# The opening of a Fourier and mixture kernel: batch 0's first stage stored and relaid in groups, half of w1 converted later

## The chip, the cores and the metric

The kernel runs on one core of a Trainium2 chip. The metric is the device time of one execution in microseconds (us). Before the change it is 980.48 us, the median of 3 runs (980.14 to 981.08).

## What is computed

```python
def _attn_ref(x):                      # x: 8 batches, 3136 positions, 256 channels
    X = np.fft.fft(x, axis=1)
    X = np.fft.fft(X, axis=2)
    return X.real.astype(np.float32)

def _moe_ref(x, g_ln, w_ch1, w_ch2):   # w_ch1: 256 x 1024, w_ch2: 1024 x 256
    mu = np.mean(x, axis=-1, keepdims=True)
    var = np.mean((x - mu) ** 2, axis=-1, keepdims=True)
    xn = (x - mu) / np.sqrt(var + 1e-06) * g_ln
    ch = np.maximum(xn @ w_ch1, 0.0) @ w_ch2
    return (x + ch).astype(np.float32)
```

The output is the second function of the first one's result. x is float32; the two weight matrices arrive as 64-bit floats.

## The kernel before

The Fourier transform over the 3136 = 49 x 64 positions is done in two steps, batch by batch, on folded input (a position and its mirror image are added), and the transform over the channels is drawn into the weights and into the residual.

**Step 1.** A batch is loaded as seven tiles `x(b, 0..6)` (`load_x`; six of 512 KB and one of 256 KB). For batch 0, DVE folds each (`fold_zw`, two additions z and w; `fold_eo` makes sum and difference of these, with which TensorE needs half as many columns), TensorE multiplies by the 128 x 128 table in `tu_s` (`step1`, L283 to L291, full float32, two records for each matmul), and ACT copies the result to `s1` (L301). `step1_ends` (L268 to L274) does the same for channel 0, whose columns come from `ends` on POOL. A partition of `s1` is one row of the table, and its free axis holds 13 slots of 256 numbers.

**Relayout.** Step 2 needs the slots along the partitions. So `store1` writes slots to `scratch` in DRAM, as [slot, row, 256], and `relayout(b, g0, g1)` (L312) reads groups g0 to g1 back as `s2`, 128 partitions of 16 slots times 8. A row of the table is r * 16 + g for group g of 16 and r of 8. Slots 13 to 15 are zeros, written by `clear_scratch`, a transfer whose rows are 8 * 3 = 24.

**Step 2.** `step2(m, part)` multiplies two groups by the table `tab_s` ("m", L345) and makes a rounded part on ACT ("h", L366), a copy ("f", L368) and the rest of the rounding on DVE ("l", L370). Batch 0's m = 0 and 1 fill the first chunk of 256 frequencies and need groups 0 to 3.

**The hidden layer.** Per step s, `moe1_a(s)` runs 6 matmuls (L390; rounded times rounded, and the two mixed products), ACT copies (L395), DVE adds and subtracts to h (L396, L397). `moe1_b(s)` rounds with the nonlinearity on ACT (L404) and takes the rest on DVE (L405). `moe2(s)` runs 12 matmuls (L440). There are eight steps to a chunk; steps 4 to 7 use w1's second half of columns, and step s uses rows 128 s of w2, so that w2's quarter n serves steps 2n and 2n + 1. From step 6 on a loop runs `moe1_b(s - 1)`, `moe1_a(s)`, listed late work, `moe2(s - 3)` and listed work after it.

**Weights.** w1 comes in four parts of 512 KB, `load_w1(n)`: n = 0, 1 are its first half of columns, 2, 3 the second. `convert_z` on ACT (L567) and `convert_m` (L558, L560), `convert_b` (L572, L573) and `finish_w1` (L601) on DVE turn 64-bit floats into float32, `gw`. `transform_w1(k, i)` (L611, 512 columns, full float32) multiplies part 2k + i into `psw[k, 0..1]`. `round_w1(k)` makes w1_hi on ACT (L619), `rest_w1(k)` subtracts it on TensorE (L624), and `rest_w1_copy(k)` makes w1_lo on ACT (L629). A quarter of w2 (`load_w2(n)`, into the place of w1's part n) is converted in the same manner (L633), rounded on ACT and its rest taken on POOL (`split_w2`, L577 and L578).

**Order.** On TensorE, ACT, DVE and POOL instructions run as the text of the opening (L720 to L861) lists them, on SP's queue of transfers as well. A transfer issued from SP or ACT uses one of eight semaphores in turn, and waits until the transfer that last used it has landed. In the opening before the change, SP loads x, w1 and tables, POOL stores tiles 0 to 4, ACT stores tiles 5 and 6 and loads the first part of the table and w2's first quarter, and SP then issues the relayouts. `warm_up` runs matmuls of zeros.

## Time and profile before

| | |
|---|---|
| median of 3 runs | 980.48 us (980.14 to 981.08) |
| the profiled execution | 980.7 us, of which the span of its instructions is 978.9 us |
| TensorE busy | 968.4 us, 99% of the span |
| DVE, ACT, POOL busy | 810.1, 531.8, 235.8 us |
| TensorE in the first four stretches of 10 us | 8.45, 8.38, 9.15, 8.49 us |
| DMA share in the same stretches | 0.80, 1.01, 0.94, 0.84 |

How to read it: PE is TensorE's matmul side and PEld its loading of weights. In a row of the timeline stand start, duration, engine, line, operation, tiles written and read, shape, the number of instructions merged, and in brackets the idle time ahead of the first and what ended it. A merged row's duration runs to the last one's modelled end, some 0.28 us after its start. The DMA share is the mean busy share of the core's 16 DMA engines.

### The profile page before, as it was taken

To read this page: it belongs to the slowest core of one execution; us is meant where nothing else is said; L and a number is where in the kernel's file an instruction comes from. 1 tells how busy PE (TensorE), PEld (TensorE's weight loads), DVE (VectorE), ACT (ScalarE), POOL (GpSimd) and SP (SyncE) were. 2 spreads that over 40 slices of the span, in tenths; PEclk is the share of its full clock that TensorE was granted. 3 is DMA by queue.
4 is the path that set the end of the run, shared out by engine and by line. 5 is a ranking of instruction groups with operands and counts; after the bars stand their busy time and mean duration, and the time that the engine had idled before them with its cause. 6 is when DMAs were issued, how large, how long until landed. Compare 5 with 4: busy or idle time off the path is not lost.

```text
span 978.9 us, 21927 instructions
## 1 busy us (share of the span) xinstructions
PE 968.4 (99%) x8365; PEld 955.6 (98%) x8366; DVE 810.1 (83%) x2194; ACT 531.8 (54%) x1416; POOL 235.8 (24%) x288
## 2 busy tenths in 40 slices
PE   8999999999999999999999999999999999999998
PEld 5899999999999999999999999999999999999998
DVE  6888878888888888888888888888888788788887
ACT  3656565555555555555555555555555655554553
POOL 2166342223223133311432143222323200000000
PEclk9999999999999999999999999999999999999999
DMA  9934442113222151221422142211311121100101
GB/s 347 331 120 141 141 136 89 64 55 146 88 87 76 45 189 66 76 77 62 161 76 74 58 157 76 98 55 66 114 55 44 44 72 76 44 22 23 45 22 45
DMA packets 40865, 92.06 MB, mean 94 GB/s; under 512 B 3984, under 2 KB 17296, under 8 KB 39736
## 3 DMA queue, kind: packets, MB, share of 16 engines
q1 hardware_dynamic: 39208, 87.72, 25.1%
q8 instruction: 67, 1.10, 0.5%
q10 hardware_dynamic: 1104, 1.52, 0.4%
q0 software_dynamic: 448, 1.41, 0.4%
q14 instruction: 38, 0.31, 0.1%
HBM read 50.53 MB, written 40.11 MB: 93 GB/s over the span
## 4 chain that ended last, share of the span: by engine, by line
PE 92%; DVE 5%; ACT 2%; DMA 1%; issue 0%; SPq 0%; ACTq 0%; DVEq 0%
PE acc L440 52%; PE ab L390 26%; PE ps L345 6%; PE psy L465 4%; PE ps L297 3%; DVE h_lo L405 1%; DMA xs<-x 1%; DVE h L396 1%; ACT h_hi L404 1%; DVE h L397 1%; PE psw L611 0%; DVE st L487 0%; DVE gw L601 0%; DVE fw L633 0%; ACT ew L567 0%
## 5 line engine op out<-in xcount | busy, mean ns | idle before, releaser
L440 PE MATMUL acc<-w_hi,h_lo 128*128 128x256 f32 x1568 | 434.3, 277 | 0.2 <-DVE h_lo L405 0.2
L440 PE MATMUL acc<-w_lo,h_hi 128*128 128x256 f32 x1568 | 434.0, 277 | 0.0
L440 PE MATMUL acc<-w_hi,h_hi 128*128 128x256 f32 x1568 | 433.9, 277 | 0.0
L404 ACT ACTIVATE h_hi<-h 128x512 fp32r<-128x512 f32 x392 | 249.8, 637 | 300.0 <-DVE h L397 299.9
L405 DVE SCALAR_TENSOR_TENSOR h_lo<-h,h_hi 128x512 fp32r<-128x512 f32 x392 | 292.2, 745 | 138.7 <-ACT h_hi L404 136.4
L440 PEld LDWEIGHTS acc<-w_hi,h_lo 128*128 128x128 f32 x1568 | 294.6, 188 | 0.7 <-DVE h_lo L405 0.4
L440 PEld LDWEIGHTS acc<-w_lo,h_hi 128*128 128x128 f32 x1568 | 294.7, 188 | 0.0
L440 PEld LDWEIGHTS acc<-w_hi,h_hi 128*128 128x128 f32 x1568 | 294.5, 188 | 0.0
L390 PE MATMUL ab<-ckl,w_hi 128*128 128x256 f32 x768 | 217.9, 284 | 2.4 <-DVE h L397 2.1
L390 PE MATMUL ab<-ckh,w_lo 128*128 128x256 f32 x768 | 213.0, 277 | 0.3 <-ACT ckh L366 0.3
L390 PE MATMUL ab<-ckh,w_hi 128*128 128x256 f32 x768 | 212.6, 277 | 0.0
L249 POOL TENSOR_TENSOR fl<-f,fh 128x512 fp32r<-128x512 f32 (+1 forms) x49 | 60.2, 1228 | 514.3 <-ACT fh L242 514.3
L397 DVE TENSOR_TENSOR h<-asb,ab 128x256 f32<-128x256 f32 x384 | 158.8, 414 | 0.0
L396 DVE TENSOR_TENSOR h<-asb,ab 128x256 f32<-128x256 f32 x384 | 158.6, 413 | 0.2 <-ACT asb L395 0.2
L390 PEld LDWEIGHTS ab<-ckl,w_hi 128*128 128x128 f32 x768 | 144.3, 188 | 3.7 <-issue 3.1
L390 PEld LDWEIGHTS ab<-ckh,w_lo 128*128 128x128 f32 x768 | 144.5, 188 | 0.5 <-ACT ckh L366 0.5
L390 PEld LDWEIGHTS ab<-ckh,w_hi 128*128 128x128 f32 x768 | 144.3, 188 | 0.0
L395 ACT COPY asb<-ab 128x256 f32<-128x256 f32 x384 | 137.9, 359 | 7.9 <-PE ab L390 1.5
L345 PE MATMUL ps<-tab_s,s 104*128 104x98 f32 (+1 forms) x512 | 66.3, 275 | 0.1
L301 ACT COPY s<-ps 128x510 f32<-128x510 f32 (+1 forms) x56 | 31.1, 555 | 58.3 <-PE ps L297 47.0
L345 PEld LDWEIGHTS ps<-tab_s,s 104*128 104x128 f32 x512 | 61.8, 192 | 0.6 <-PE pw L718 0.6
L366 ACT CAST ckh<-ps 128x392 fp32r<-128x392 f32 (+49 forms) x112 | 39.7, 356 | 36.9 <-PE ps L345 36.6
(112 smaller groups left out, 942.6 us busy)
## 6 DMA issues: line engine op xcount, KB each, us to landing
xs<-x SPq DMA_DIRECT2D x48, 512.0 KB, 4.6
out<-o SPq DMA_DIRECT2D x96, 256.0 KB, 2.0
s<-scratch SPq DMA_DIRECT2D x7, 2048.0 KB, 8.2
scratch<-s SPq DMA_DIRECT2D x42, 256.0 KB, 2.3
w1p_all<-w SPq DMA_DIRECT2D x7, 512.0 KB, 9.1
xs<-x SPq DMA_DIRECT2D x8, 256.0 KB, 3.1
scratch<-s POOLq DMA_DIRECT2D x5, 256.0 KB, 7.5
s<-scratch SPq DMA_DIRECT2D x1, 1024.0 KB, 8.3
```

Source lines behind the costliest of these rows:

```text
L249: nc.gpsimd.tensor_tensor(out=lo, in0=f, in1=hi.bitcast(F32), op=ALU.subtract)
L301: nc.scalar.copy(s[:, :, :255], ps.rearrange("p a h d -> p a (h d)")[:, :, :255])
L345: nc.tensor.matmul(ps[:, h, k0 - base:k1 - base], s2[b][:KP, g, 128 * h:128 * h + 128], tab_s[:KP, h, k0:k1], start=(h == 0 and g == 2 * j ...
L366: nc.scalar.copy(hi, src)
L390: nc.tensor.matmul(pt, wt[wi][:, j, fs], ch[xi][:, j, :w], start=(n == 0), stop=(n == 2))
L395: nc.scalar.copy(asb[:, :w], pa)
L396: nc.vector.tensor_tensor(out=h[:, :w], in0=asb[:, :w], in1=pb, op=ALU.add)
L397: nc.vector.tensor_tensor(out=h[:, w:], in0=asb[:, :m], in1=pb[:, :m], op=ALU.subtract)
L404: nc.scalar.activation(h_hi, h, AF.Relu)
L405: nc.vector.scalar_tensor_tensor(out=h_lo, in0=h, scalar=0.0, in1=h_hi.bitcast(F32), op0=ALU.max, op1=ALU.subtract)
L440: nc.tensor.matmul(acc[c, i][:, side], hs[xi][:, h0:h0 + 128], ws[wi][:, f], start=(f == 0 and side == 0 and n == 0), stop=(f == 7 and n = ...
L465: nc.tensor.matmul(ps[:, j, :n], ck[:, j], ty_s[:, j, :n], start=(j == 0), stop=True, skip_group_check=True)
```

## The change

The columns of the three 128 x 128 tables in `tu` are permuted for batch 0, so that row g * 8 + r of step 1's result belongs to group g: a group is then 8 neighbouring partitions of `s1`. A new function `store_groups(i, g0, g1)` stores groups g0 to g1 of one slot in a transfer. Batch 0's tiles are stored for groups 0 to 3 first, from SP instead of POOL and ACT, and the two relayouts of these groups follow; groups 4 to 15 are stored after them. w1's parts 2 and 3 are loaded, converted and transformed later: part 3 is loaded behind the first relayouts, and `transform_w1(1, 0)` and `(1, 1)` stand between the first hidden steps. w2's first quarter is loaded from SP and converted ahead of step 2. Tile 6 of batch 0 no longer goes through `fold_eo`. Later batches use the old order of columns, which ACT and DVE restore in the loop's steps 12 and 13.

```diff
@@ -86,6 +86,7 @@
         tu[s, 256 + 64 * par:320 + 64 * par] = th
         tu[s, 384 + 2 * par] = 1.0
         tu[s, 385 + 2 * par] = np.cos(np.pi * np.arange(64))
+    tu[:, :384] = tu[:, :384].reshape(128, 3, 8, 16).transpose(0, 1, 3, 2).reshape(128, 384)
     vs = [(par, v[v >= 0]) for par, v in enumerate(slots())]
     tab = np.zeros((2, 2, 2, NS, 2, HALF))
     tz = np.zeros((4, NS, 50))
@@ -265,7 +266,8 @@
         alloc1(b)
         n = p1 - p0
         ps = psum.tile([128, 2, n], F32, tag="y" if b else "fft", name=f"pse{p0}_{b}")
-        nc.tensor.matmul(ps[:, 0], tu_s[:, 256:384], e0c[b][:, p0:p1], start=True, stop=True)
+        th = tu_s[:, 128:256] if b else tu_s[:, 256:384]
+        nc.tensor.matmul(ps[:, 0], th, e0c[b][:, p0:p1], start=True, stop=True)
         if p1 == NS:
             nc.tensor.matmul(ps[:KP, 1, 0:1], masked, one, start=False, stop=True,
                              skip_group_check=True)
@@ -304,6 +306,12 @@
         s = s1[b][:, 2 * i:2 * i + len(held(i))]
         in_order(eng.dma_start(scratch[b][2 * i:2 * i + len(held(i))].rearrange("s p d -> p s d"),
                                s.rearrange("p a h d -> p a (h d)")))
+
+    def store_groups(i, g0, g1, eng=nc.sync):
+
+        for s in held(i):
+            eng.dma_start(scratch[0][s].rearrange("(r g) d -> g r d", g=16)[g0:g1],
+                          s1[0][8 * g0:8 * g1, s].rearrange("p h d -> p (h d)"))
 
     def relayout(b, g0=0, g1=16, eng=nc.sync):
         if b not in s2:
@@ -728,137 +736,145 @@
             nc.scalar.dma_start(tu_s, tu)
             load_x(0, 0)
             nc.scalar.activation(one, one, AF.Sqrt)
-            for i in range(1, 4):
-                load_x(0, i)
+            load_x(0, 1)
+            load_x(0, 2)
             load_w1(0)
-            for i in (4, 5, 6):
+            for i in range(3, NU):
                 load_x(0, i)
             load_w1(1)
             nc.sync.dma_start(tw_all, tw)
             nc.sync.dma_start(tz_s, tz)
+            nc.sync.dma_start(tab_s[:, :, :gb[4]], tab[:, :, :gb[4]])
             load_w1(2)
-            load_w1(3)
             clear_scratch(0, nc.gpsimd, 0, 2)
             nc.gpsimd.memset(zmu, 0.0)
             nc.gpsimd.memset(masked, 0.0)
             ends(0, 0, 6)
-            for i in range(3):
-                fold_zw(0, i, nc.vector)
-                step1(0, i)
+            fold_zw(0, 0, nc.vector)
+            step1(0, 0)
+            fold_zw(0, 1, nc.vector)
+            step1(0, 1)
+            convert_z("w1_0", w1p[0])
+            fold_zw(0, 2, nc.vector)
+            step1(0, 2)
+            convert_m("w1_0", w1p[0])
             step1_ends(0, 0, 6)
             for i in range(3):
-                store1(0, i, nc.gpsimd)
+                store_groups(i, 0, 4)
             fold_zw(0, 3, nc.vector)
-            convert_z("w1_0", w1p[0])
             step1(0, 3)
+            convert_b("w1_0")
+            load_w2(0)
             ends(0, 6, 10)
             ends(0, 10, NS)
-            convert_m("w1_0", w1p[0])
+            convert_z("w1_1", w1p[1])
             fold_zw(0, 4, nc.vector)
-            convert_b("w1_0")
+            step1(0, 4)
             nc.vector.tensor_scalar_mul(g_s, tu_s[:, 388:390], 2.0 ** -20)
             finish_w1(0)
-            step1(0, 4)
             step1_ends(0, 6, 10)
-            store1(0, 3, nc.gpsimd)
-            store1(0, 4, nc.gpsimd)
-            for i in (5, 6):
-                fold_zw(0, i, nc.vector)
-                fold_eo(0, i, nc.vector)
+            store_groups(3, 0, 4)
+            store_groups(4, 0, 4)
+            fold_zw(0, 5, nc.vector)
+            fold_eo(0, 5, nc.vector)
             step1(0, 5)
+            fold_zw(0, 6, nc.vector)
+            step1_ends(0, 10, NS)
+            store_groups(5, 0, 4)
+            step1(0, 6)
+            store_groups(6, 0, 4)
+            relayout(0, 0, 2)
+            relayout(0, 2, 4)
+            load_w1(3)
             convert_m("w1_1", w1p[1])
-            step1_ends(0, 10, NS)
-            store1(0, 5, nc.scalar)
-            convert_z("w1_1", w1p[1])
             convert_b("w1_1")
             finish_w1(1)
-            step1(0, 6)
-            store1(0, 6, nc.scalar)
-            nc.scalar.dma_start(tab_s[:, :, :gb[4]], tab[:, :, :gb[4]])
-            load_w2(0, nc.scalar)
+            load_w2(1)
+            for i in range(NU):
+                store_groups(i, 4, 16)
+            clear_scratch(0, nc.sync, 2, 8)
+            relayout(0, 4, 8)
+            nc.sync.dma_start(tab_s[:, :, gb[4]:gb[8]], tab[:, :, gb[4]:gb[8]])
+            relayout(0, 8, 16)
+            nc.scalar.copy(minus, tw_all[:, 512:])
+            convert_z("w2_0", w2p[0])
+            transform_w1(0, 0)
+            transform_w1(0, 1)
+            convert_m("w2_0", w2p[0])
+            convert_b("w2_0")
+            f0 = finish_w2(0)
+            round_w1(0)
             convert_z("w1_2", w1p[2])
-            nc.scalar.copy(minus, tw_all[:, 512:])
-            convert_z("w1_3", w1p[3])
             convert_m("w1_2", w1p[2])
             convert_b("w1_2")
             finish_w1(2)
+            warm_up(2, warm_h)
+            step2(0, "m")
+            step2(0, "h")
+            step2(0, "l")
+            rest_w1(0)
+            rest_w1_copy(0)
+            step2(1, "m")
+            step2(1, "h", 0)
+            step2(1, "l", 0)
+            load_w2(2)
+            split_w2(0, f0)
+            moe1_a(0, ((0, 0), (1, 0), (0, 1)))
+            moe1_a(1, ((0, 0), (1, 0), (0, 1)))
+            moe1_b(0)
+            transform_w1(1, 0)
+            convert_z("w1_3", w1p[3])
+            moe1_b(1)
             convert_m("w1_3", w1p[3])
-            relayout(0, 0, 2)
-            relayout(0, 2, 4)
-            load_w2(1)
-            clear_scratch(0, nc.sync, 2, 8)
-            load_w2(2)
-            relayout(0, 4, 8)
-            nc.sync.dma_start(tab_s[:, :, gb[4]:gb[8]], tab[:, :, gb[4]:gb[8]])
-            relayout(0, 8, 16)
-            transform_w1(0, 0)
-            transform_w1(0, 1)
-            round_w1(0)
-            convert_b("w1_3")
             load_w2(3)
             nc.sync.dma_start(ty_s, ty)
             nc.sync.dma_start(tab_s[:, :, gb[8]:], tab[:, :, gb[8]:])
             for i in range(NU):
                 load_x(1, i)
             clear_scratch(1, nc.sync)
+            moe1_a(2)
+            moe2(0)
+            convert_b("w1_3")
             finish_w1(3)
-            transform_w1(1, 0)
-            rest_w1(0)
-            convert_z("w2_0", w2p[0])
-            rest_w1_copy(0)
+            convert_z("w2_1", w2p[1])
+            moe1_a(3)
+            moe1_b(2)
+            moe2(1)
+            convert_m("w2_1", w2p[1])
             transform_w1(1, 1)
             round_w1(1)
-            convert_m("w2_0", w2p[0])
-            convert_b("w2_0")
-            f0 = finish_w2(0)
-            split(t1_hi, t1_lo, tu_s[:, 0:128])
-            warm_up(2, warm_h)
-            step2(0, "m")
-            step2(0, "h")
-            step2(0, "l")
-            step2(1, "m")
-            step2(1, "h", 0)
-            step2(1, "l", 0)
-            convert_z("w2_1", w2p[1])
-            convert_m("w2_1", w2p[1])
             convert_b("w2_1")
             f = finish_w2(1)
-            moe1_a(0, ((1, 0), (0, 0), (0, 1)))
-            split_w2(0, f0)
-            moe1_a(1, ((1, 0), (0, 0), (0, 1)))
             rest_w1(1)
-            moe1_b(0)
+            rest_w1_copy(1)
             split_w2(1, f)
-            moe1_a(2)
-            moe1_b(1)
-            moe1_a(3)
-            moe1_b(2)
-            rest_w1_copy(1)
-            convert_z("w2_2", w2p[2])
-            convert_m("w2_2", w2p[2])
+            moe1_b(3)
+            moe1_a(4)
             step2(0, "f")
             step2(1, "f")
             step2(1, "hl", 1)
-            moe2(0)
-            moe1_b(3)
-            moe2(1)
-            moe1_a(4)
+            convert_z("w2_2", w2p[2])
+            convert_m("w2_2", w2p[2])
             convert_b("w2_2")
             f = finish_w2(2)
             nc.gpsimd.tensor_scalar(out=neg, in0=ty_s[:, 1, 129:130], scalar1=2.0, scalar2=-1.0,
                                     op0=ALU.mult, op1=ALU.add)
+            moe2(2)
             step2(2, "m")
             moe1_b(4)
             moe1_a(5)
             split_w2(2, f)
             step2(2, "hf")
             step2(2, "l")
-            moe2(2)
             convert_z("w2_3", w2p[3])
             convert_m("w2_3", w2p[3])
             add_late(6, convert_b, "w2_3")
             add_late(6, lambda: w2f.append(finish_w2(3)))
             late[7].insert(0, (lambda: split_w2(3, w2f.pop()), ()))
+            add_late(12, nc.scalar.copy, tu_s[:, 128:256].rearrange("p (r g) -> p r g", r=8),
+                     tu_s[:, 256:384].rearrange("p (g r) -> p r g", r=8))
+            add_late(13, split, *(t.rearrange("p (r g) -> p r g", r=8) for t in (t1_hi, t1_lo)),
+                     tu_s[:, 0:128].rearrange("p (g r) -> p r g", r=8))
 
         main.append(True)
         lag, last = 3, 8 * NCH
```

## The prediction

> **What bounds the kernel now.** I read the busy times first, then the stretches of the opening, then TensorE's own order of time with the idle time ahead of each group, then SP's queue.
>
> ```profile
> span 978.9 us, 21927 instructions
> PE 968.4 (99%) x8365; PEld 955.6 (98%) x8366; DVE 810.1 (83%) x2194; ACT 531.8 (54%) x1416; POOL 235.8 (24%) x288
> ...
> 10.00:20.00 10.00, 8.38 (x40) 6.23 (x38) 7.80 (x23) 4.09 (x11) 5.20 (x9) 1.00 1.01 384
> 200.00:900.00 700.00, 700.00 (x6185) 700.00 (x6184) 582.85 (x1585) 384.69 (x1031) 160.68 (x194) 1.00 0.22 80
> ```
>
> The columns of a stretch are PE, PEld, DVE, ACT, POOL busy, clock, DMA share, GB/s. From 200 to 900 us TensorE (PE) has no gap, so the end moves only by PE work added or removed and by PE idle time in the opening. There the DMA engines are full (share 1.01 at 384 GB/s). PE's gaps:
>
> ```profile
> 16.20 1.10 PE L283 MATMUL ps<-f,tu_s 128*128 128x256 f32 x4 [1.19 <-DVE f L236]
> 17.98 1.02 PE L611 MATMUL psw<-gw,tw_all 128*128 128x512 f32 x2
> 19.43 3.17 PE L611 MATMUL psw<-gw,tw_all 128*128 128x512 f32 x6 [0.43 <-ACT s L301]
> 23.27 1.99 PE L611 MATMUL psw<-gw,tw_all 128*128 128x512 f32 x4 [0.68 <-DVE gw L601]
> 24.70 1.03 PE L624 MATMUL psw<-w_hi,minus 128*128 128x512 f32 x2
> 25.66 1.98 PE L611 MATMUL psw<-gw,tw_all 128*128 128x512 f32 x4
> 28.14 0.69 PE L345 MATMUL ps<-tab_s,s 104*128 104x99 f32 x4
> 30.89 0.39 PE L390 MATMUL ab<-ckh,w_lo 128*128 128x256 f32 x1 [0.35 <-ACT ckh L366]
> 34.28 0.36 PE L390 MATMUL ab<-ckl,w_hi 128*128 128x256 f32 x1 [1.16 <-DVE h L397]
> 39.53 1.03 PE L345 MATMUL ps<-tab_s,s 104*128 104x98 f32 x8
> 50.32 0.36 PE L390 MATMUL ab<-ckl,w_hi 128*128 128x256 f32 x1 [0.23 <-DVE h L397]
> 57.80 0.36 PE L390 MATMUL ab<-ckl,w_hi 128*128 128x256 f32 x1 [0.76 <-DVE h L397]
> ```
>
> The listed gaps are 4.8 us in all, and all the change can win. The point to see: while the relayout is awaited (18 to 28 us) PE is not idle. It transforms w1 (L611); the rows at 23.27 and 25.66 are w1's second half.
>
> ```profile
> SPq L312 <- DMA scratch<-s: 11.0, 2, 10.8
> SPq L587 <- DMA xs<-x: 3.5, 2, 2.5
> 23.99 0.81 SPq L312 DMA_DIRECT2D s<-scratch  x2
> s<-scratch SPq DMA_DIRECT2D x2, 256.0 KB, 4.0
> ```
>
> SP waits 10.8 us for the stores and issues the relayout at 23.99; step 2 (L345) starts at 28.14.
>
> **The change, part by part.** Write T for step 2's first matmul, 28.14 now.
>
> *When the stores land.* Ahead of the relayout the transfers now carry (code sizes, KB) tu 195, x 3328, w1 2048, tw and tz 345, stores 1664, the clear 96, table 393: 8069. At 384 GB/s that is 21.5 us, so 2.5 us of the 23.99 are start and landing. After the change w1 is 1536 and the stores 416, while the load of w2's first quarter (512), which SP now issues between store 2 and store 3, stands ahead: 6821. Spread evenly that would take 18.2 us. But a piece of the new stores has four groups outermost, 32 rows of 1 KB. No row shows such a transfer; the nearest is the clear of 24 rows (L256, issued at 25.39):
>
> ```profile
> 31.00:31.50 0.50, 0.50 (x4) 0.48 (x5) 0.49 (x2) 0.48 (x1) 0.00 (x0) 1.00 0.75 291
> ```
>
> While its last part runs with the load behind it, the share is 0.75: 12 engines of 16, so a transfer is dealt in equal parts by its outer count. Between four engines and sixteen I take four, the equal parts of four groups. Each of 13 pieces is then 8 KB on the same four engines, at 24 GB/s each (384/16) 0.34 us, 4.4 us for all 13, in one queue with everything else. The other 6405 KB take 17.1 us; sum 21.5, plus 2.5: 24.0, the time of now. SP is also in order, and an issue waits for an old transfer to land (L587 above), so store 3 waits for w1's third load: I take 24.5.
>
> [...]
>
> *Flight.* Now 28.14 − 23.99 = 4.15 us, with a load of w2 ahead of it; the bound from below is the 2.3 us of a store of the same size:
>
> ```profile
> scratch<-s SPq DMA_DIRECT2D x42, 256.0 KB, 2.3
> ```
>
> I take 3.2. T = 27.7, gain 0.4 us.
>
> *PE work that loses its cover.* transform_w1(1, ·) moves behind step 2, into a PE that is then full: the rows at 23.27 and 25.66, each four records 0.43 apart, 1.7 each: +3.4 us. rest_w1(0) and its copies also go behind step2(0). Now 2.75 us pass from L345 to the first L390; then it is
>
> ```profile
> 26.84 1.06 ACT L629 CAST w_lo<-psw 128x512 fp32r<-128x512 f32 x2
> 29.53 0.48 ACT L366 CAST ckh<-ps 128x390 fp32r<-128x390 f32 x1 [0.46 <-PE ps L345]
> 30.58 0.26 ACT L366 CAST ckh<-ps 128x122 fp32r<-128x122 f32 x1 [0.57 <-PE ps L345]
> ```
>
> 1.39 to the first cast, 0.48, the two copies 1.06, 0.26, 0.05: 3.25, so +0.5.
>
> *Conversions behind step 2.* w1_3 and w2_1 are then converted on DVE between the hidden layers, with these durations:
>
> ```profile
> 31.52 0.69 DVE L560 SCALAR_TENSOR_TENSOR fw<-w1p_all,mw 128x512 f32<-128x512 uint32 x1
> 33.72 0.41 DVE L397 TENSOR_TENSOR h<-asb,ab 128x256 f32<-128x256 f32 x1
> 34.84 0.69 DVE L405 SCALAR_TENSOR_TENSOR h_lo<-h,h_hi 128x512 fp32r<-128x512 f32 x1
> 32.97 1.63 POOL L578 TENSOR_TENSOR w_lo<-fw,w_hi 128x512 fp32r<-128x512 f32 x1 [15.50 <-ACT w_hi L577]
> 35.39 1.30 POOL L578 TENSOR_TENSOR w_lo<-fw,w_hi 128x512 fp32r<-128x512 f32 x1 [0.79 <-ACT w_hi L577]
> ```
>
> Counted from T: moe1_a(0) at 3.25, h(0) and h(1) on DVE until 6.0, h_lo(1) waits for ACT until 7.9; convert_m 1.1, h(2) 0.7, convert_b 0.65, finish 0.75 give gw3 at 11.05. PE has done moe1_a(0..3), transform(1, 0), moe2(0..1) by 10.65: idle 0.4. transform(1, 1) ends at 12.8; rest_w1(1) and moe1_a(4) wait for ACT's rounding and copies, 0.85 more. DVE needs h(3), h_lo(2) and w2_1's 2.4 us: 14.7; ACT's cast 0.6 and POOL's split 1.3 (1.63 at most) end at 16.8; moe2(2), which PE reaches at 14.9, waits 1.8. That is 3.05 of idle time in place of the 1.16 at 34.28 and 0.35 of the smaller waits: I take +1.4 (0 if DVE keeps ahead, 3 if the lag is carried on).
>
> *Clock.* After the first half's transform PE is done at some 22.2 us: w1_1 has landed in time, DVE is free after the folds at 16.4 and gives gw1 2.5 us later, at 18.9; step 1 ends at 18.3 (17.98 now, and 0.43 more, below), then two transforms of 1.7 each, the second with its warm-ups to 22.2. Up to T it is idle for 5 us.
>
> ```profile
> 1.49 3.78 PE L718 MATMUL pw<-warm 128*128 128x512 f32 x4 [1.49 <-DVE warm L725]
> 975.17 0.28 PE L440 MATMUL acc<-w_hi,h_hi 128*128 128x256 f32 x1
> 977.00:978.00 1.00, 0.00 (x0) 0.00 (x0) 0.00 (x0) 0.00 (x0) 0.00 (x0) 1.00 0.24 81
> 978.00:979.00 1.00, 0.00 (x0) 0.00 (x0) 0.00 (x0) 0.00 (x0) 0.00 (x0) 0.78 0.00 0
> ```
>
> The granted clock falls about 3.4 us after the last matmul, and the first warm-ups ran at some 0.85 us a record against 0.43 later. A gap of 5 us would so start step 2 at half clock: its first ten records go from 0.107 (the row at 39.53: 1.03 less a tail of 0.28, over 7) to 0.16 (98 columns of 512, of 0.85): +0.55, the rest and the next eight add as much: +1.0, between 0 (gap too short) and 2.4 (hidden layers too).
>
> [...]
>
> *Edits with no price.* Tile 6 without fold_eo: eight records of 0.107 for four, +0.43 on PE, less 0.5 on DVE ahead of it. The split of t1 moved into the loop: 0.33 on ACT and 0.29 on DVE, under a PE that has work queued; 0.3 if not. x of batch 1 comes some 2 us later, as the loop does. Thirteen pieces at 0.35 of issue keep SP 5 us ahead of the third and fourth relayout, due 18 us after T.
>
> Sum: −0.4 + 3.4 + 0.5 + 1.4 + 1.0 = +5.9 on the profiled execution's 980.7 (its span plus 1.8 outside), which is 0.2 above the median: 986.4 on the median's scale.
>
> **Rivals.** 1. *Even spread.* If the pieces use all engines, the last one is bound by SP: step 1's last copy ends at about 18.6 (19.37 now, behind a conversion of 0.66 on ACT), SP issues seven pieces from 19.0, landing at 23.2; T = 23.2 + 2.6 = 25.8. −2.3 + 3.4 + 0.5 + 1.4, no half clock: +3.0, 983.5. For it: the bytes fit; against it: the 0.75.
>
> ```profile
> 19.02 0.35 ACT L301 COPY s<-ps 128x255 f32<-128x255 f32 x1
> ```
>
> 2. *Faster.* Landing at 22.2 and 2.3 of flight give T = 24.5 (−3.6); the second half of w1 fills PE's gaps, 34.28 included, so that +3.9 of work comes with 1.7 less idle, and the DVE waits at 50.32 and 57.80 (1.0) vanish as well: −2.4, 978.1. It decides where T falls below 25.0. For it: 1250 KB fewer stores; against it: DVE's 7.9 and 16.8 above.
>
> 3. *No gain that shows.* T near 25 with half of those waits: −3.1 + 3.9 − 0.8 = 0, 980.5.
>
> **How the numbers follow.** The forecast has 0.45, the even spread 0.25, no change 0.12, faster 0.18. Within 0.2% (about 2 us, what a measurement of this kernel can tell from no change) lies rival 3 alone, so slower has 0.70. The likeliest case's own range is 983 to 990 (clock 0 to 2.4, conversions 0 to 3); for 8 in 10 the range reaches down to 979, leaving out most of the faster case, and up to 989.5.
>
> **What would show it.** In the changed profile: SP's s<-scratch issue at 24 to 25.5 and L345 at 27 to 28.5; L611 records behind L345; a granted clock below 1.00 between 24 and 32; a gap of PE at an L440 group that waits for POOL's w_lo; DMA share near 0.25 while the pieces go. L345 before 25.5 with share above 0.8 makes the forecast wrong, and PE gaps after T of less than 2 us in all would, too.

## The result, and the profile after

The changed kernel takes 992.15 us (median of 4 runs, 991.37 to 993.2) against 980.57 us for the kernel before (980.14 to 981.08): a ratio of 1.0115, with a 95% interval of 1.0103 to 1.0127, or 11.6 us slower. The forecast was slower, 986.4 us, with 989.5 as the upper end.

The busy times of the changed kernel, and its stretches (columns as before: PE, PEld, DVE, ACT, POOL, clock, DMA share, GB/s):

```profile
span 989.6 us, 21958 instructions
PE 973.4 (98%) x8372; PEld 960.4 (97%) x8372; DVE 810.1 (82%) x2192; ACT 532.6 (54%) x1417; POOL 231.6 (23%) x283
...
24.00:28.00 4.00, 0.00 (x0) 0.00 (x0) 2.95 (x6) 0.51 (x1) 0.00 (x0) 0.92 0.39 113
28.00:32.00 4.00, 3.50 (x14) 3.33 (x15) 0.52 (x1) 1.03 (x3) 0.00 (x0) 0.50 0.99 308
32.00:36.00 4.00, 3.65 (x17) 3.40 (x17) 0.40 (x3) 1.67 (x5) 1.27 (x1) 0.50 0.68 223
36.00:40.00 4.00, 4.00 (x19) 2.77 (x19) 3.18 (x8) 2.24 (x5) 0.00 (x0) 0.80 0.57 146
200.00:900.00 700.00, 700.00 (x6184) 700.00 (x6183) 584.51 (x1591) 383.18 (x1025) 163.12 (x196) 1.00 0.23 80
```

The first of these stretches in the kernel before:

```profile
24.00:28.00 4.00, 3.95 (x10) 1.45 (x10) 3.17 (x9) 1.74 (x4) 0.00 (x0) 1.00 0.88 259
```

From 200 to 900 us TensorE is busy without a gap in both kernels, so the 10.7 us of the longer span (989.6 against 978.9) are lost in the opening. TensorE has no matmul from 24 to 28 us, where the kernel before had 3.95 us of them, and then works at half the clock until 37.59 us. TensorE's order of time in the changed kernel (L353 is the old L345, L398 the old L390, L448 the old L440, L619 the old L611):

```profile
18.40 3.60 PE L619 MATMUL psw<-gw,tw_all 128*128 128x512 f32 x8
28.50 1.15 PE L353 MATMUL ps<-tab_s,s 104*128 104x99 f32 x4 [6.08 <-DMA s<-scratch]
33.84 0.58 PE L398 MATMUL ab<-ckh,w_hi 128*128 128x256 f32 x1 [0.35 <-ACT ckh L374]
36.57 2.39 PE L619 MATMUL psw<-gw,tw_all 128*128 128x512 f32 x4
42.89 1.88 PE L619 MATMUL psw<-gw,tw_all 128*128 128x512 f32 x4
45.45 0.50 PE L632 MATMUL psw<-w_hi,minus 128*128 128x512 f32 x1 [0.36 <-ACT w_hi L627]
48.48 0.39 PE L448 MATMUL acc<-w_lo,h_hi 128*128 128x256 f32 x1 [0.96 <-POOL w_lo L586]
53.61 1.06 PE L473 MATMUL psy<-ty_s,ck 128*128 128x129 f32 x8
55.27 0.35 PE L398 MATMUL ab<-ckl,w_hi 128*128 128x256 f32 x1 [0.60 <-DVE h L405]
58.60 0.36 PE L398 MATMUL ab<-ckl,w_hi 128*128 128x256 f32 x1 [1.04 <-DVE h L405]
```

The moved transform stands at 36.57 and 42.89. After 48 us these rows show three gaps (0.96, 0.60, 1.04), two of them behind DVE. SP's queue and the one long wait of DVE behind it:

```profile
12.48 5.26 SPq L313 DMA_DIRECT2D scratch<-s  x6
19.06 4.50 SPq L313 DMA_DIRECT2D scratch<-s  x7
25.29 0.82 SPq L320 DMA_DIRECT2D s<-scratch  x2
27.11 10.27 SPq L313 DMA_DIRECT2D scratch<-s  x13
41.02 0.36 SPq L320 DMA_DIRECT2D s<-scratch  x1
42.78 1.40 SPq L600 DMA_DIRECT2D w1p_all<-w  x2
44.23 0.94 SPq L830 DMA_DIRECT2D ty_s<-ty  x1
```

```profile
51.44 0.43 DVE L566 TENSOR_SCALAR mw<-w1p_all 128x512 int32<-128x512 int32 x1 [1.45 <-DMA w1p_all<-w]
```

and in SP's queue of the kernel before:

```profile
26.00 0.41 SPq L592 DMA_DIRECT2D w1p_all<-w  x1
31.96 0.33 SPq L312 DMA_DIRECT2D s<-scratch  x1
```

A piece is one transfer of `store_groups`. The thirteen pieces of groups 4 to 15 hold SP from 27.11 to 37.38 us, 0.79 each. The third relayout, which also waits 1.0 us for the pieces and 1.8 us for the transfer of `clear_scratch` behind them to land, goes out at 41.02 instead of 31.96. w2's part 2 goes out at 42.78 instead of 26.00, for two reasons: the change puts its load behind the fourth relayout, where the kernel before has it ahead of the third, and the pieces stand ahead of all of these. Its first conversion on DVE starts at 51.44, when it has landed. Two candidates, then: the half clock, and SP's queue.

### The profile page after: what moved, and what is told of

The parts are those of the page before. It is cut to its first block, busy times and chain, and to the rows that moved or that the text cites. A ratio compares the mean times of both kernels' runs of the same rounds, so it can differ in the third digit from the quotient of the medians.

```text
span 989.6 us, 21958 instructions
## 1 busy us (share of the span) xinstructions
PE 973.4 (98%) x8372; PEld 960.4 (97%) x8372; DVE 810.1 (82%) x2192; ACT 532.6 (54%) x1417; POOL 231.6 (23%) x283
## 4 chain that ended last, share of the span: by engine, by line
PE 90%; DVE 4%; DMA 3%; SPq 1%; ACT 1%; issue 0%; DVEq 0%; ACTq 0%
PE acc L448 51%; PE ab L398 26%; PE ps L353 5%; PE psy L473 4%; PE ps L299 3%; DMA w1p_all<-w 1%; SPq L313 1%; DMA tw_all<-tw 1%; DVE h_lo L413 1%; DMA xs<-x 1%; DVE h L404 0%; DVE h L405 0%; ACT h_hi L412 0%; DMA scratch<-warm 0%; DVE st L495 0%
## 5 line engine op out<-in xcount | busy, mean ns | idle before, releaser
L448 PE MATMUL acc<-w_lo,h_hi 128*128 128x256 f32 x1568 | 433.2, 276 | 1.0 <-POOL w_lo L586 1.0
L448 PE MATMUL acc<-w_hi,h_lo 128*128 128x256 f32 x1568 | 433.4, 276 | 0.2 <-DVE h_lo L413 0.2
L448 PE MATMUL acc<-w_hi,h_hi 128*128 128x256 f32 x1568 | 433.1, 276 | 0.0
L448 PEld LDWEIGHTS acc<-w_lo,h_hi 128*128 128x128 f32 x1568 | 294.5, 188 | 1.2 <-POOL w_lo L586 1.2
L448 PEld LDWEIGHTS acc<-w_hi,h_lo 128*128 128x128 f32 x1568 | 294.4, 188 | 0.8 <-DVE h_lo L413 0.4
L448 PEld LDWEIGHTS acc<-w_hi,h_hi 128*128 128x128 f32 x1568 | 294.4, 188 | 0.0
L398 PE MATMUL ab<-ckl,w_hi 128*128 128x256 f32 x768 | 218.3, 284 | 2.6 <-DVE h L405 2.4
L398 PE MATMUL ab<-ckh,w_hi 128*128 128x256 f32 x768 | 212.9, 277 | 0.3 <-ACT ckh L374 0.3
L398 PE MATMUL ab<-ckh,w_lo 128*128 128x256 f32 x768 | 213.2, 278 | 0.1
L404 DVE TENSOR_TENSOR h<-asb,ab 128x256 f32<-128x256 f32 x384 | 158.7, 413 | 2.4 <-ACT asb L403 2.4
L398 PEld LDWEIGHTS ab<-ckl,w_hi 128*128 128x128 f32 x768 | 144.8, 188 | 4.0 <-issue 2.6
L398 PEld LDWEIGHTS ab<-ckh,w_lo 128*128 128x128 f32 x768 | 145.0, 189 | 0.7 <-ACT w_lo L637 0.5
L398 PEld LDWEIGHTS ab<-ckh,w_hi 128*128 128x128 f32 x768 | 144.7, 188 | 0.6 <-ACT ckh L374 0.6
L353 PE MATMUL ps<-tab_s,s 104*128 104x98 f32 (+1 forms) x512 | 68.0, 279 | 6.1 <-DMA s<-scratch 6.1
L353 PEld LDWEIGHTS ps<-tab_s,s 104*128 104x128 f32 x512 | 63.7, 196 | 6.7 <-issue 6.5
```

The source lines that it names most:

```text
L353: nc.tensor.matmul(ps[:, h, k0 - base:k1 - base], s2[b][:KP, g, 128 * h:128 * h + 128], tab_s[:KP, h, k0:k1], start=(h == 0 and g == 2 * j ...
L398: nc.tensor.matmul(pt, wt[wi][:, j, fs], ch[xi][:, j, :w], start=(n == 0), stop=(n == 2))
L404: nc.vector.tensor_tensor(out=h[:, :w], in0=asb[:, :w], in1=pb, op=ALU.add)
L448: nc.tensor.matmul(acc[c, i][:, side], hs[xi][:, h0:h0 + 128], ws[wi][:, f], start=(f == 0 and side == 0 and n == 0), stop=(f == 7 and n = ...
```

## The experiments

The theories were: A, the half clock alone carries the loss; C, SP's queue and the late transfers behind it; B, the later half of w1 costs by itself, through the transform without cover and the half clock. In the expectations of e1 and e2, B still stands for the conversions behind step 2; D is POOL's own work, E and F say that the moved half of w1 costs everything or nothing. The later parts of the table `tab_s` are called sampled rows, `ty_s` the selector, and both together the constants. Each run's time stands beside runs of the kernel before on the same chip (medians of 980.5 to 980.9 us); the rows shown are those of one profiled execution. In the code, `...` stands for further lines.

**e1_warm: only the clock.**

```diff
-            warm_up(2, warm_h)
+            warm_up(26, warm_h)
             step2(0, "m")
```

> The changed kernel with 26 warm-up matmuls of zeros instead of 2 ahead of step 2, so that PE's gap of 6.1 us before step 2 falls below 1 us; nothing else. Theory A (half clock): in the changed kernel the clock fell at 27.35 us and came back only at 37.59, and the work in between took about 4 us longer; with the gap filled the granted clock stays 1.00 and the time falls by 3.3 to 4.2 us, to about 988.3. Theory B (conversions): behind step 2 PE follows DVE and ACT anyway, and a fast clock only makes the later gaps longer: under 1 us, 991.2 or more.

Measured: 993.13 us (991.12 to 993.35), ratio 1.0119 [1.0104, 1.0134]; no gain. TensorE's order of time, and DVE's:

```profile
28.29 0.66 PE L353 MATMUL ps<-tab_s,s 104*128 104x99 f32 x4 [0.89 <-DMA s<-scratch]
44.86 0.39 PE L448 MATMUL acc<-w_lo,h_hi 128*128 128x256 f32 x1 [0.96 <-POOL w_lo L586]
53.44 2.07 PE L473 MATMUL psy<-ty_s,ck 128*128 128x129 f32 x8 [2.27 <-DMA ty_s<-ty]
```

```profile
51.00 0.43 DVE L566 TENSOR_SCALAR mw<-w1p_all 128x512 int32<-128x512 int32 x1 [4.64 <-DMA w1p_all<-w]
```

The clock was 1.0 until 53.5 us and TensorE came to the same matmul 3.62 us earlier (44.86 for 48.48), and then met the late transfers: DVE's wait for w2's part 2 grew from 1.45 to 4.64 us and ended at 51.00, 0.4 earlier. The time is the one that the rival named (991.2 or more), but TensorE did run ahead, which the rival did not expect. Theory A falls: behind the half clock stood something just as late.

**e2_early and e3_spread: a better filled gap, and pieces dealt evenly.** e2 puts w1's part 2 ahead of step 2 again; e3 lays scratch out so that a piece is one run of rows.

```diff
 e2:
...
             transform_w1(0, 1)
+            convert_m("w1_2", w1p[2])
+            convert_b("w1_2")
+            finish_w1(2)
+            round_w1(0)
+            transform_w1(1, 0)
...
```

```diff
 e3:
...
-            eng.dma_start(scratch[0][s].rearrange("(r g) d -> g r d", g=16)[g0:g1],
+            eng.dma_start(scratch[0][s, 8 * g0:8 * g1],
...
```

> The changed kernel with w1's part 2 converted and transformed ahead of w2's first quarter and ahead of step 2, in the time in which DVE waits for w2 (18.4 to 22.3 us) and PE for the relayout; part 3 stays behind step 2. Theory A: 1.7 us of PE work regains its cover, and PE's gap shrinks from 6.1 to about 4.5 us: 990.4 if the clock still falls, 986.5 if it does not. Theory B: DVE and ACT behind step 2 lose nothing but the conversion they never waited for: at most 1 us, 991.2.

> The changed kernel with the scratch of batch 0 laid out by pairs of groups, so that a piece is 32 neighbouring rows of 1 KB in DRAM (outer count 32, not 4), and the relayout reads each pair by a transfer of its own, with the same 2 KB rows. If the outer count of 4 costs (on four engines, and 0.58 us of SP time each): pieces go out in about 0.35 us, all engines share them, the relayout is issued at 23.5 instead of 25.3 and step 2 starts near 26.8; the gap is then some 4.4 us, the 12 later groups are stored some 5 us sooner: 990.0 with the fall of the clock, 986.3 without. If instead the write to DRAM and its 2 us of latency set the time: step 2 at 28 or later, 991.5 or more.

Measured: e2 993.13 us (991.53 to 994.67), e3 991.37 (990.23 to 992.79); ratios 1.0124 [1.0109, 1.0139] and 1.0107 [1.0092, 1.0122]. In e2 part 2's transform shortened the gap ahead of step 2 from 6.08 to 4.27 us, and the clock still halved (28.67 to 42.32 us). In e3 the relayout went out at 23.93 and step 2 began at 27.48, 1.02 us earlier; the half clock and the queue stayed. Both times lie above what was expected with the half clock (990.4 and 990.0):

```profile
26.31 10.56 SPq L318 DMA_DIRECT2D scratch<-s  x13
```

**e4_w22: an earlier load of w2's part 2.**

```diff
+            load_w2(2)
             for i in range(NU):
                 store_groups(i, 4, 16)
...
```

> The changed kernel with the load of w2's third quarter issued ahead of the 13 stores of groups 4 to 15, not behind the last relayout. In the changed kernel DVE waited 1.45 us and ACT 2.4 us for it at 51.4 us, and PE's gaps of 0.60 at 55.27 and 1.04 at 58.60 came after that. If that wait is what they come from: 1.0 to 1.6 less, 990.8. If DVE is behind anyway: 0 to 0.4, 992.

Measured: 993.95 us (992.88 to 994.7), ratio 1.0135 [1.0118, 1.0152]. This load goes to the place of w1's part 2, and in the text it now stands ahead of that part's conversion, so that the part is replaced by w2's values and its conversion waits for them; TensorE waited 3.91 us for ACT ahead of the first hidden layer. The run says nothing on the theories. What it does not show is that the load has to be late: in the changed kernel DVE reads w1's part 2 for the last time at 25.05 to 25.74 us (L568), ahead of the first piece at 27.11. With the pieces moved behind that conversion and behind the load, the load could, by these rows, go out some 15 us earlier in the same place. That order was not tried.

**e5_pool and e6_pool_warm: the later pieces from POOL.** (e6 with the 26 warm-ups as well.)

```diff
-                store_groups(i, 4, 16)
+                store_groups(i, 4, 16, nc.gpsimd)
```

> The changed kernel, with the stores of groups 4 to 15 of batch 0 issued by POOL instead of SP. In the changed kernel SP spends 10.27 us on these thirteen pieces (0.79 each), and the transfers queued behind them (third and fourth relayout, sampled rows, part 2 of w2, selector, x of batch 1) come some 9 us later than in the kernel before. Theory C (SP's queue): these transfers come back to within 2 us of where the kernel before has them; the half clock from 27 to 37 us stays and costs TensorE some 4 us, so about 990 us, and 986.5 if that half clock turns out to be hidden. Rival A (the half clock alone carries the loss): 992 us as in the changed kernel, however early the transfers come. Rival D (POOL's own work, delayed by some 10 us of issuing, becomes the wait): 992 us or more, with TensorE waiting for POOL's conversions ahead of the experts of the opening.

> As the run before it (stores of groups 4 to 15 on POOL), with 26 dummy matmuls instead of 2 at each warm-up of the opening. With the warm-up alone TensorE was 3.6 us earlier by 45 us and lost it again at 53.4 us, waiting for the selector's transfer. Theory C with A (SP's late transfers and the half clock, either of which hides the gain of removing the other): 986 us, 3 to 5 us under the run before it. Rival A alone: the same as with the warm-up alone, 992 to 993. Rival C alone: the same time as the run before it. Rival D (POOL): TensorE waits for POOL's conversions, 990 us or more.

Measured: 993.22 us (991.78 to 994.53) and 991.02 (990.93 to 992.02); ratios 1.0126 [1.011, 1.0141] and 1.0103 [1.0086, 1.012]. None of the theories expected what POOL did in e5:

```profile
14.85 4.53 POOL L313 DMA_DIRECT2D scratch<-s  x8
20.22 2.82 POOL L313 DMA_DIRECT2D scratch<-s  x5 [0.84 <-DMA scratch<-s]
```

POOL waited little (0.84 us) and sent the pieces out while the first groups were still being stored. The first relayout left SP at 27.75 (28.06 in e6) instead of 25.29, and step 2 began at 30.89 (31.21). The third relayout went out at 37.35 (37.42) instead of 41.02, but the start was late: the two runs tried another kernel than they were meant to.

**s1_late_w1 and s1_warm: the later half of w1 alone,** on whole-tile stores and unpermuted columns, without and with the 26 warm-ups. The rest of the change stays (the order of the loads, w2's first quarter early, tile 6 without `fold_eo`), and is counted with it. Against the changed kernel:

```diff
...
             for i in range(3):
-                store_groups(i, 0, 4)
+                store1(0, i, nc.gpsimd)
...
-            for i in range(NU):
-                store_groups(i, 4, 16)
...
```

> The kernel before, with only the later conversion of half of w1: step 1's columns are as before, batch 0 is stored whole tile by whole tile from POOL and ACT and relaid out after the last. No thirteen pieces on SP. Theory C with A: SP's transfers stay where the kernel before has them; what is left is the conversion and the transform behind step 2, and a gap of TensorE ahead of step 2 as wide as before or wider; 984 us, and up to 988 if the clock halves in it. Rival E (the moved half of w1 carries the whole loss): 990 to 992 us. Rival F (the moved half of w1 costs nothing): 980.5.

> The later conversion of half of w1 alone (989.3 us, 8.5 over the kernel before, granted clock 0.5 from 25.8 to 36.1 us), now with 26 dummy matmuls at each warm-up so that the clock has no reason to fall. Theory B (two parts: w1's transform no longer fills TensorE's gap ahead of step 2, 4 us or so, and the half clock, 4 us or so): clock 1.0 until 40 us, and 985 us, some 4 under the run without the warm-ups. Rival (the moved half of w1 costs all 8.5 by the order of its conversions, the half clock is hidden): 989 us again.

Measured: 989.29 us (988.27 to 990.55), ratio 1.0086 [1.0071, 1.0101]; with the warm-ups 986.63 (985.6 to 987.33), ratio 1.0057 [1.0042, 1.0072]. s1_late_w1's start of step 2 and a stretch behind it:

```profile
27.57 1.15 PE L352 MATMUL ps<-tab_s,s 104*128 104x99 f32 x4 [5.29 <-issue]
```

```profile
28.00:32.00 4.00, 4.00 (x19) 3.81 (x19) 0.56 (x1) 1.55 (x3) 0.00 (x0) 0.50 0.91 307
```

and s1_warm's second half of the transform with the two gaps that follow it:

```profile
33.19 1.88 PE L618 MATMUL psw<-gw,tw_all 128*128 128x512 f32 x4
39.42 1.98 PE L618 MATMUL psw<-gw,tw_all 128*128 128x512 f32 x4
42.08 0.50 PE L631 MATMUL psw<-w_hi,minus 128*128 128x512 f32 x1 [0.36 <-ACT w_hi L626]
45.12 0.58 PE L447 MATMUL acc<-w_lo,h_hi 128*128 128x256 f32 x1 [0.96 <-POOL w_lo L585]
```

Theory B holds in its two parts: with the warm-ups the later half of w1 costs some 5.7 us (986.63 − 980.91), and the half clock 2.7 more. Without the pieces w2's part 2 goes out at 36.15 in s1, and DVE does not wait for it. I had expected 984 of s1, and 988 if the clock halved, which it did: the half clock's price was still too low. Note that whole tiles bring step 2 to 27.57, earlier than the groups ahead do (28.50).

**s2_groups and s5_dup: the pieces without the later w1.** s2 has the permuted columns and the grouped stores on the kernel before; s5 has nothing of the change but thirteen added transfers of the pieces' shape in SP's queue (96 KB each in rows of 1 KB, not of the 508 bytes that its expectation names), into a buffer that is overwritten later:

```diff
 s5:
             load_w2(1)
+            for i in range(NU):
+                for s in held(i):
+                    nc.sync.dma_start(scratch[1][s].rearrange("(r g) d -> g r d", g=16)[4:16],
+                                      s1[0][0:96, s].rearrange("p h d -> p (h d)"))
             clear_scratch(0, nc.sync, 2, 8)
```

> The kernel before, with the permuted columns and the grouped stores of batch 0 from SP (groups 0 to 3 first, thirteen pieces for the others), but w1 converted and transformed as in the kernel before. Theory C: the thirteen pieces hold SP for some 10 us, the selector's transfer lands at about 53 us, where the kernel before uses it at 44.7; about 989.5 us, 8 to 10 us over the kernel before. Rival E (the moved half of w1 carries the loss): 980 to 982 us. Rival A (half clock): TensorE keeps w1's transform as cover in the gap, the clock stays full, and the time is within 2 us of the kernel before.

> The kernel before with nothing of the change, and thirteen transfers of the pieces' shape (12 groups of 8 rows of 508 bytes each) added to SP's queue at the place where the changed kernel has its pieces; they write to batch 1's scratch, which batch 1 overwrites later, so nothing reads them. Columns, stores, relayouts and w1 stay as they were. Theory C (SP's queue by itself): 10 us of issue, the selector lands at about 52 us where the kernel before uses it at 44.7, and the time is 6 to 9 us over the kernel before, 987 to 990. Rival (SP has 8 us to spare here, and the changed kernel's transfers are late for another reason): 981 us.

Measured: s2 992.66 us (991.93 to 992.99), ratio 1.0119 [1.0104, 1.0134]; s5 987.91 (987.36 to 988.33), ratio 1.007 [1.0055, 1.0085]. s5's queue, and TensorE:

```profile
25.66 11.04 SPq L791 DMA_DIRECT2D scratch<-s  x13
```

```profile
28.64 0.69 PE L345 MATMUL ps<-tab_s,s 104*128 104x99 f32 x4
...
46.77 2.00 PE L345 MATMUL ps<-tab_s,s 104*128 104x98 f32 x8 [6.81 <-DMA tab_s<-tab]
```

s5 starts step 2 at 28.64, 0.5 us after the kernel before; then TensorE waits 6.81 us for sampled rows that stand behind the pieces, and the kernel is 7.0 us longer. This shows the queue's cost by itself, with what the wait brings along: the clock is at half from 44.66 to 51.48. s2 missed its 989.5 and loses more, since the first groups' pieces are also late there: step 2 begins at 32.14, with the clock halved from 30.45 to 40.69 and again from 47.51 to 57.75, and the same wait for sampled rows is 5.80.

**g1_ahead and g2_ahead_warm: the constants ahead of the thirteen pieces.** (g2 with the warm-ups.)

```diff
+            nc.sync.dma_start(tab_s[:, :, gb[4]:gb[8]], tab[:, :, gb[4]:gb[8]])
+            nc.sync.dma_start(ty_s, ty)
+            nc.sync.dma_start(tab_s[:, :, gb[8]:], tab[:, :, gb[8]:])
             for i in range(NU):
                 store_groups(i, 4, 16)
...
```

> The changed kernel, with the loads of the sampled rows' later parts and of the selector (three transfers that depend on nothing) ahead of the thirteen pieces in SP's queue. The half clock from 27 to 37 us stays. Theory C+A: the wait for the selector at 53.6 us is gone, TensorE is bound by its own work as in the run with late w1 alone: 989.5 to 990.5. Rival (the late selector is no cause, what counts is x of batch 1 or part 2 of w2): 992 us, as the changed kernel.

> The run before it with 26 dummy matmuls at each warm-up as well: neither the half clock nor the wait for the selector. With the warm-ups alone TensorE came to the product with part 0 of w2 at 44.86 us, 3.6 us earlier than the changed kernel, and then waited 0.81 for sampled rows and 2.27 for the selector. Theory C+A: both waits gone, 986.5 us (985.5 to 988), that is, what the prediction's sum gave. Rival (another late transfer behind the pieces, the third relayout or part 2 of w2, takes their place): 990 us or more.

Measured: 992.64 us (992.24 to 992.89) and 992.4 (992.21 to 992.94); ratios 1.0118 [1.0103, 1.0133] and 1.0116 [1.0099, 1.0132]. My expectation missed and the rivals hold. The waits for the selector are gone, and in g2 two others stand there, on TensorE and on DVE:

```profile
48.81 1.10 PE L353 MATMUL ps<-tab_s,s 104*128 104x98 f32 x8 [2.05 <-DMA s<-scratch]
```

```profile
52.55 0.43 DVE L566 TENSOR_SCALAR mw<-w1p_all 128x512 int32<-128x512 int32 x1 [5.82 <-DMA w1p_all<-w]
```

The selector was a symptom. The wait that counts is DVE's, for w2's part 2: DVE works in order, so the next h of the hidden layer (L404, at 55.48) is queued behind that conversion, which starts at 52.55.

**g3_two and g4_two_warm: a shorter queue.** On e3's order of scratch, both samples of a tile go in one transfer: 7 pieces ahead and 7 behind (g4 with the warm-ups). Against e3:

```diff
-        for s in held(i):
-            eng.dma_start(scratch[0][s, 8 * g0:8 * g1],
-                          s1[0][8 * g0:8 * g1, s].rearrange("p h d -> p (h d)"))
+        n = len(held(i))
+        eng.dma_start(scratch[0][2 * i:2 * i + n, 8 * g0:8 * g1].rearrange("s p d -> p s d"),
+                      s1[0][8 * g0:8 * g1, 2 * i:2 * i + n].rearrange("p a h d -> p a (h d)"))
```

> The changed kernel with its scratch of batch 0 in an order in which a piece is one run of rows (the spread tried before), and both samples of a tile in one transfer: 7 pieces ahead and 7 behind instead of 13 and 13. The clock is left as it is. Theory C+A (SP's queue and the half clock, whichever is later): SP is through with the later pieces by 33 us instead of 37.4, the waits for sampled rows and selector are gone, the half clock of some 10 us stays; 988 to 989.5 us, as the run with late w1 alone (989.3). Rival (the late pieces' own bytes hold the transfers behind them, however few the issues): third relayout at 40 us again, 991 to 992 us.

> The run before it with 26 dummy matmuls at each warm-up: in the changed kernel itself neither the half clock nor the long queue. Theory C+A: 985.5 to 986.6 us, as late w1 alone with the warm-ups (986.6) or as much less as step 2 starts earlier; what is left is w1's transform that no longer fills TensorE's gap. Rival (permuted columns and groups ahead cost something of their own): 989 us or more.

Measured: 988.14 us (987.4 to 988.81) and 988.49 (987.67 to 988.62); ratios 1.0074 [1.0059, 1.0089] and 1.0076 [1.0061, 1.0091]. In g3:

```profile
24.81 0.66 PE L363 MATMUL ps<-tab_s,s 104*128 104x99 f32 x4 [2.97 <-DMA s<-scratch]
48.80 1.16 PE L483 MATMUL psy<-ty_s,ck 128*128 128x129 f32 x8 [2.19 <-DMA ty_s<-ty]
```

```profile
47.06 0.43 DVE L576 TENSOR_SCALAR mw<-w1p_all 128x512 int32<-128x512 int32 x1 [4.18 <-DMA w1p_all<-w]
```

Step 2 begins at 24.81, which is what the change was after, and in this execution the clock stays full until 50.98 without warm-ups. All of it is lost again: DVE waits 4.18 us for w2's part 2, now landing at 47.06. The execution shown is one of four: its mean clock is 0.998, while the other three have 0.992 to 0.994, which is some 12 to 16 us at half clock in all, and still take only 0.7 to 1.4 us more. So g4's warm-ups have little to win; they also hold TensorE until step 2, which starts at 27.08 there. DVE still waits 2.49 us for w2's part 2 (47.66), g4 is no faster, and its expectation missed for the reason of g2.

**g6_two_consts and g8_consts_warm: and the constants loaded earlier still,** ahead of the first relayouts (g8 with the warm-ups).

```diff
...
             store_groups(6, 0, 4)
+            nc.sync.dma_start(tab_s[:, :, gb[4]:gb[8]], tab[:, :, gb[4]:gb[8]])
+            nc.sync.dma_start(ty_s, ty)
+            nc.sync.dma_start(tab_s[:, :, gb[8]:], tab[:, :, gb[8]:])
             relayout(0, 0, 2)
...
```

> The changed kernel with seven pieces ahead and seven behind (988.1 us; step 2 at 24.8 us, the clock full until 51 us, then a wait of 2.19 us for the selector at 48.8), now with the sampled rows' later parts and the selector loaded ahead of the first relayouts, where SP waits for the last pieces from 19 to 21 us anyway. Theory (the start of step 2 at 24.8 is worth 2 to 4 us once nothing late stands behind it): 984 to 985.5 us. Rival (part 2 of w2 or the third relayout takes the selector's place, as when the loads were put just ahead of the thirteen pieces): 987.5 to 988.5 us, with DVE's h as the wait around 52 us.

> The changed kernel with seven pieces ahead and seven behind and the constants ahead of the first relayouts (991.9 us: no wait for a transfer behind step 2 any more, but step 2 at 28.7 us after 6.7 us without a matmul, and the granted clock 0.5 from 26.0 to 39.7 us), now with 26 dummy matmuls at each warm-up. Theory (of the changed kernel's loss only w1's transform without its cover is left): clock 1.0 until 45 us, step 2 at 28.5, and 986 to 987 us, as late w1 alone with the warm-ups (986.6) and as the prediction's sum (986.4). Rival (the half clock is hidden behind a transfer that the profile does not show as a wait): 990 us or more.

Measured: g6 991.92 us (990.98 to 992.81), ratio 1.0116 [1.0102, 1.0129]; g8 987.13 (986.5 to 992.59), ratio 1.0079 [1.0062, 1.0096]. g6 missed in the other direction. Its relayouts go out at 21.34 as in g3, but the constants' bytes are ahead of them (DMA share 1.03 from 24 to 28 us):

```profile
28.72 1.15 PE L363 MATMUL ps<-tab_s,s 104*128 104x99 f32 x4 [6.67 <-issue]
```

so that the gap is long again and the clock is 0.5 from 26.02 to 39.67. No wait for a transfer is left behind it: DVE is ready for w2's part 2 only at 51.06. This run has the queue's waits away and the half clock left, as e1 had the reverse, and like e1 it gains nothing. g8 takes the half clock away as well: step 2 at 27.59, and

```profile
46.84 0.43 DVE L576 TENSOR_SCALAR mw<-w1p_all 128x512 int32<-128x512 int32 x1 [1.17 <-DMA w1p_all<-w]
```

4.8 us less than g6 and 5.0 less than the changed kernel: in the changed kernel itself, with both the long queue and the half clock gone, what is left is what late w1 alone costs (986.63). The prediction's sum of 986.4 is near, but counts +1.0 for a half clock behind step 2 that g8's profile does not have. The warm-ups did not always hold the clock: one of g8's six executions took 992.59 us with a mean clock of 0.993, where g6 has 0.991 to 0.993, and the other five 986.5 to 988.65 with 0.997 to 1.000.

**g5_two_early and g7_early_consts: the groups ahead without the later w1,** in the cheap form of g3, on the kernel before, first groups from POOL and ACT; g7 loads the constants earlier as g6 does.

> The kernel before with w1 as it was, and the groups ahead in their cheap form: permuted columns, one run of rows and one transfer per tile, the first four groups from POOL and ACT where whole tiles went before, the other twelve from SP behind the first relayouts. Theory (groups ahead gain nothing here, since TensorE is busy with w1's transform until 28 us and so step 2 can't start earlier, and cost nothing once the queue is short): 980.5 to 982 us. Rival (the later pieces still push the third relayout, due at 46 us, past its use): 984 us or more. Rival (the earlier relayout pays): below 979.5.

> The kernel before with the cheap groups ahead and w1 as it was (982.5 us, with waits of 1.35 us for sampled rows at 40.2 and 0.43 for the selector at 45.9), now with these loads ahead of the first relayouts. Theory (the two waits are the whole cost of the groups ahead, and their gain is the 0.5 us by which step 2 starts earlier): 980.0 to 981 us, the kernel before within what can be told. Rival (third relayout or part 2 of w2 comes too late instead): 982.5 us again.

Measured: g5 982.54 us (981.67 to 983.86), ratio 1.0017 [1.0007, 1.0026], 0.5 over its range; g7 980.67 (979.96 to 981.83), ratio 1.0001 [0.9992, 1.001]. g5 waits for its late constants:

```profile
40.20 1.10 PE L363 MATMUL ps<-tab_s,s 104*128 104x98 f32 x8 [1.35 <-DMA tab_s<-tab]
```

and with these early the groups ahead cost nothing and gain nothing: TensorE has w1's transform to do until step 2 begins at 28 us, and an earlier relayout only waits for it. No version that I tried beats the kernel before.

## Why the prediction was wrong in size

One milestone orders the runs: the time at which DVE begins to convert w2's part 2. Thirteen kernels have the changed kernel's order of conversions (all but s2, s5, g5, g7, e2 and e4), and from that time to the end of the span they take 937.7 to 939.9 us, while the milestone itself moves by 6.75 us. So what a kernel loses, it has lost by then, within these 2.2 us. Eight of them, each by its profiled execution:

| kernel | DVE is ready | conversion starts | span | long half clock, from some 26 us |
|---|---|---|---|---|
| changed kernel | 49.99 | 51.44 | 989.6 | yes |
| e1 (clock) | 46.36 | 51.00 | 989.3 | no |
| g2 (clock, constants) | 46.73 | 52.55 | 991.1 | no |
| g3 (short queue) | 42.88 | 47.06 | 985.6 | no |
| g6 (short queue, constants) | 51.06 | 51.06 | 991.0 | yes |
| g8 (short queue, constants, clock) | 45.67 | 46.84 | 984.8 | no |
| s1 (late w1 alone) | 48.83 | 48.83 | 986.5 | yes |
| s1_warm | 46.55 | 46.55 | 985.4 | no |

"Ready" is the start less the wait for the transfer. The start is the later of two paths: TensorE, ACT and DVE's own work, which the half clock sets back by 3.6 us, and the landing of w2's part 2, which its place behind SP's pieces sets back to 51. In the changed kernel the two are 1.45 us apart, and therefore taking one away gains next to nothing (e1 for the clock, g6 for the queue) and taking both gains 5.0 (g8).

Point by point:

- *The landing and the flight: near in size, and four engines as forecast.* SP issued the relayout at 25.29 (24.5 forecast), the flight was 3.21 us (3.2), step 2 began at 28.50 (27.7, so +0.4 and not −0.4). From 21 to 24 us the DMA share was 0.26, 0.27 and 0.26: some four engines of sixteen (0.26 times 16 is 4.2). With 32 rows outermost (e3) the relayout went out 1.36 us earlier; part of that is SP's, whose issues of a piece fell from 0.58 us and more to 0.30 to 0.42, so that its last went out 0.8 us earlier (22.16 against 22.98). With four engines the forecast took these issues as no limit. That equal parts follow the outer count was its estimate, from one share of 0.75 with 24 rows; the pieces of four groups add 0.26, and no run shows the share of another count alone. Rival 1 was wrong on the spread.
- *The transform without cover, the rest and the conversions: the total near, in part by luck.* The forecast's 3.4 + 0.5 + 1.4 are 5.3; late w1 alone with the warm-ups measured 5.7 (4.1 to 7.1 by its interval). The conversions' +1.4 of idle time did not come: from step 2 to 200 us TensorE is busy 168.85 of 171.46 us in s1_warm and 169.12 of 171.86 in the kernel before, 2.6 and 2.7 us idle. Instead s1_warm starts step 2 0.4 us later and has a stretch of 3.41 us at half clock. The gap of TensorE for POOL's w_lo came as named, 0.96 us, and smaller than the 1.8 taken.
- *The first step that failed, the clock: the right mechanism, a term too small.* Forecast were +1.0, by eighteen records of step 2 at half clock, and 2.4 as the bound. It stayed at half for 10.2 us, until 9.1 us after step 2 had begun; the first hidden layer came 5.34 us after it (3.25 forecast). By the warm-ups it is worth 3.6 us to DVE (49.99 against 46.36), 2.7 in s1 and 4.8 in g6, where step 2 also began 1.1 us later.
- *The second step that failed: "Thirteen pieces at 0.35 of issue keep SP 5 us ahead of the third and fourth relayout, due 18 us after T".* The prediction names no row for 0.35, which is near the cheapest issues on SP's queue before the change (0.33), and it was less than half of the price: 0.79 each, 10.27 in all. And the list of who stands behind them stopped at the relayouts. These were in time, as TensorE read them from 49.88 on without a wait. Behind them stand sampled rows, w2's part 2 and 3 and the selector, and w2's part 2 is due at 46 us. The edit stood under "no price", and alone on the kernel before it costs 7.0 us (s5).
- *Either step alone was enough to miss:* 993.13 us with the clock held and the queue as it is (e1), 991.92 with the queue's waits gone and the half clock left (g6), both above the range. And every sign that the prediction named came: the issue, step 2's start, L611's rows behind it (L619 now), the clock, the gap for w_lo and the share. None of them concerned the queue behind the relayouts or how long the half clock lasts, so they could not tell the sum from this result. (The full DMA engines that it mentions, share 1.01, are those of 10 to 20 us, not of 200 to 900.)
- *Rivals 2 and 3* needed step 2 near 25 us. g3's profiled execution has it there and no long half clock, and g3 is still 7.3 us slower than the kernel before (988.14 against 980.8), with DVE waiting 4.18 us. Without that wait its 42.88 and the 937.7 to 939.9 us behind it would give a span of 980.6 to 982.8, still above 978.9; this is an estimate, which no run shows.

The sum without its clock term, 985.4, stands 1.2 to 1.7 us under s1_warm and g8. Both profiled executions still have one stretch of 3.41 us at half clock, at 45.0 and 44.4 us, which is at most 1.7 us of work. In s1_warm this is most of the difference: its two executions with a mean clock of 1.000 took 985.6 and 986.07 us, the two with 0.998 took 987.2 and 987.33. g8's do not sort in this way (987.0 with 1.000, 986.5 with 0.997). Why a piece takes 0.79 us was not settled: as 12 groups of 8 rows (10.27) and as one run of 96 rows (10.56) the thirteen take the same, but in the first form each holds SP for 0.73 to 0.81 us with no wait for a semaphore between them, and in the second for 0.30 to 1.11 with pauses of up to 1.6 us. Seven of twice the size take 6.53 (g3) and 5.26 (g5).

## What to carry to other kernels

Before a batch of transfers is put into a queue that works in order, as SP's did here (thirteen pieces held it for 10.27 us), list everything behind it up to the first consumer that waits, with its due time, and price the batch by an issue of the same queue and form. Where two delays run side by side, a run that takes away one shows nothing; make the run that takes away both before either is acquitted, and look for the wait that moves from one name to another (selector, relayout, w2's part). When a load into a shared place is moved, look up when that place comes free. And work that fills a gap kept the clock up here as well (1.00 from 24 to 28 us in the kernel before, 0.50 from 28 to 36 in the changed one): moving it out cost the work, 5.7 us in s1_warm, and then the work behind the gap at half speed, 2.7 more in s1.
